# Pulling the second attention forward and laying the weights' pieces along both attentions

One core of one Trainium2 chip; the metric is the device time of one launch in microseconds (us), median of several runs.

## The reference

Four batches of 1088 tokens with 4 heads of 32 go through a polynomial-sketch attention and then through a mixing over tokens. Cut to what matters:

```python
def phi(x):                                  # 8 x 8 products of two sketches
    a = np.einsum('rd,bhsd->bhsr', S1, x)
    b = np.einsum('rd,bhsd->bhsr', S2, x)
    return np.einsum('bhsi,bhsj->bhsij', a, b).reshape(*x.shape[:-1], r * r)
q_p, k_p = phi(q), phi(k)
num = np.einsum('bhsf,bhfd->bhsd', q_p, np.einsum('bhsf,bhsd->bhfd', k_p, v))
den = np.einsum('bhsf,bhf->bhs', q_p, np.sum(k_p, axis=2))[..., None] + 1e-06
x = num / den                                # then, heads side by side:
theta = x @ w_theta
y = einsum('ts,bsd->btd', w_tok_r, x*cos(theta)) + einsum('ts,bsd->btd', w_tok_i, x*sin(theta))
u = x + y
out = u + maximum(u @ w_ch, 0)
```

Two 1088 x 1088 token weights are needed by every mixing. They arrive as 64-bit floats in 34 pieces of 128 x 544.

## The kernel before

A scheduler puts each engine's instructions in an order by the levels' priorities and its own estimates of time; the program text only gives dependencies and priorities. A piece of the weights takes one transfer, three ScalarE passes and two VectorE instructions:

```python
        A.activation(dst, hi.bitcast(F32), AF.Copy, scale=2.0**-112)
        A.activation(step[:, :, 1].bitcast(F16), hi.bitcast(F32), AF.Copy, scale=2.0**-60)
        A.activation(step[:, :, 0], lo.bitcast(U32), AF.Copy, scale=2.0**-29)
        ts(x, x, 3, ALU.logical_shift_left)
        tt(V, x, x, step.rearrange("p n t -> p (n t)").bitcast(I32), ALU.add)
```

An attention is, in this order of data: powers of keys and queries (a maximum over the block, a trip through TensorE and back), slices of keys and queries, a small matrix, `features` (`lv`), `denominators` (first instruction `fl`, last `rd`), and for each of three token groups the query product `qp`, its transposes and products on TensorE, `x`, and cosine and sine parts `z`. The level "first" goes before "weights", and "attention" after it:

```python
    with level("weights"):
        for i in range(NK):
            for n in range(0, S, PIECE):
                load_f32(wT[:, i, n:n + PIECE], w_tok[i][:, n:n + PIECE])
    # ... cut ...
    with level("first"):
        # ... constants, first keys ...   (cut)
        attention(0)
    with level("attention"):
        keys(1)
        attention(1)
        keys(2)
    mixing(0, True)                       # all three token groups at once
    # ... mixings 1 to 3 between attentions 2 and 3 (cut)
```

Of the kernel before, what the change touches and what calls it, by code (L numbers as in the profile page):

```python
# [21 lines left out]
F32 = mybir.dt.float32  # L22
F16 = mybir.dt.float16
# [15 lines left out]
TINY = 2.0**-60  # L39
PIECE = 544  # L40
# [3 lines left out]
def kernel(  # L44
# [46 lines left out]

    def tt(eng, o, a, b, op):
        eng.tensor_tensor(out=o, in0=a, in1=b, op=op)  # L93

    def ts(o, a, s1, op0, s2=None, op1=None):
        kw = {} if op1 is None else {"op1": op1}
        V.tensor_scalar(out=o, in0=a, scalar1=s1, scalar2=s2, op0=op0, **kw)  # L97

    def stt(o, a, s, b, op0, op1):
        V.scalar_tensor_tensor(out=o, in0=a, scalar=s, in1=b, op0=op0, op1=op1)  # L100

# [16 lines left out]
    def load_f32(dst, src):  # L118
# [13 lines left out]
        step = stg.tile([P, PIECE, 2], I16, tag="step", name="step", bufs=2)[:p, :n]  # L132
# [4 lines left out]
        ts(x, x, 3, ALU.logical_shift_left)  # L137
        tt(V, x, x, step.rearrange("p n t -> p (n t)").bitcast(I32), ALU.add)

    def load_pair(src, n, tag, copies=1):  # L140

        p = src.shape[0]
        m = p * copies
        hi = const.tile([P, n], F32, tag=f"{tag}_hi", name=f"{tag}_hi")[:m]
        lo = const.tile([P, n], F32, tag=f"{tag}_lo", name=f"{tag}_lo")[:m]
        if src.dtype == F32:
            for i in range(copies):
                nc.sync.dma_start(hi[i * p:(i + 1) * p], src)
            V.memset(lo, 0.0)
            return hi, lo  # L150
        st = const.tile([P, n], I64, tag=f"{tag}_st", name=f"{tag}_st")[:m]
        for i in range(copies):
            nc.scalar.dma_start(st[i * p:(i + 1) * p], src)
        wl, wh = split(st)
        x = magnitude(hi, wh)
        y = const.tile([P, n], I32, tag=f"{tag}_y", name=f"{tag}_y")[:m]
# [4 lines left out]
        z = const.tile([P, n], I32, tag=f"{tag}_z", name=f"{tag}_z")[:m]  # L161
# [29 lines left out]
    def absmax(o, a, axis=AX.X):  # L191
        V.tensor_reduce(out=o, in_=a, axis=axis, op=ALU.max, apply_absolute_value=True)

# [25 lines left out]
    def cut4(dst, x0, rest, c0, c1, near=1, p=P):  # L219
# [3 lines left out]
        r = sm.tile([P, (B - 1) * P], F32, tag="cut_r", name="cut_r", bufs=1)[:p, :n]  # L223
        z = sm.tile([P, (B - 1) * P], F32, tag="cut_z", name="cut_z", bufs=1)[:p, :n]
# [19 lines left out]
    def spread(m, cs, z):  # L244

        o = m[:, :, cs].rearrange("p l (h r) -> p l h r", h=H)
        for o_, z_, f in ((o[:, 0:4], z, hmf[:, 0:4]), (o[:, 4:6], z[:, 0:2], hmf[:, 4:6])):
            n = o_.shape[1]
            tt(V, o_, z_.unsqueeze(2).to_broadcast([P, n, H, R]),
               f.unsqueeze(3).to_broadcast([P, n, H, R]), ALU.mult)  # L250
# [14 lines left out]
    for b in range(B):  # L265
# [6 lines left out]


    def keys_slices(b):

        kn = tiles["k", b]
# [4 lines left out]
        tt(V, ipk[:, b, 1], ip, ip, ALU.mult)  # L281

# [31 lines left out]
    def keys_matrix(bs, cm):  # L314
# [48 lines left out]
        cut4([nz[:, i].rearrange("p b r -> p (b r)") for i in range(NL)], nl[:, 0], by_level(nl), *UNIT)  # L363
        for i, b in enumerate(bs):
            spread(mv[b], slice(2 * HR, 3 * HR), nz[:, :, i])
# [4 lines left out]
        ts(g[:, 0], g[:, 0], sab[:, 0:1], ALU.mult)  # L370

    def keys_values(b, pool=(ps_acc, "acc")):

        kn, vn = tiles["k", b], tiles["v", b]
        kv = psum(*pool)[:, :4 * D].rearrange("p (n d) -> p n d", n=2)
        for g in range(NG):
# [10 lines left out]
            ks = work.tile([P, CH, 2 * R], F32, tag="ks", name="ks")  # L387
            A.copy(ks.rearrange("p n r -> p (n r)"), kf)
            kp = work.tile([P, CH, R, R], F32, tag="feat", name="kp")
# [9 lines left out]
        for j in range(2):  # L399
            pj = slice(j * R * R, (j + 1) * R * R)  # L400
            A.copy(kvbd[b][pj, :, j * D:(j + 1) * D], kv[pj, :, j * D:(j + 1) * D])
# [4 lines left out]
    def query_slices(b):  # L406

# [7 lines left out]
        tiles["qs", b] = qs  # L415
        qx = work.tile([P, NC * P], F32, tag="qx", name="qx", bufs=1)
        sl = [work.tile([P, NC * P], F16, tag=f"q{i}", name=f"q{i}", bufs=1) for i in range(3)]
        half = work.tile([P, NC * P], F16, tag="half", name="half", bufs=1)
        for g in range(NG):
            tr = psum(ps_w, "w")  # L420
# [6 lines left out]
        ts(sl[0], qx, 1.5 * 2.0**24, ALU.add, 1.5 * 2.0**24, ALU.subtract)  # L427
        tt(V, qx, qx, sl[0], ALU.subtract)
        ts(half, qx, 1.5 * 2.0**12, ALU.add, 1.5 * 2.0**12, ALU.subtract)
        A.activation(sl[1], half, AF.Copy, scale=2.0**10)  # L430
        tt(V, qx, qx, half, ALU.subtract)
        A.activation(sl[2], qx, AF.Copy, scale=2.0**10)
        tiles["qsl", b] = sl

    def features(b):

        sl, m = tiles["qsl", b], mv[b]
        lv = work.tile([P, NL, 3, NC, HR], F32, tag="lv", name="lv", bufs=1)
        W = 3 * HR
        for c in range(NC):  # L440
            lp = psum(ps_w, "w")[:, :NL * W]
            q0, q1, q2 = (x[:, c * P:(c + 1) * P] for x in sl)
            flat = m.rearrange("p l n -> p (l n)")
            nc.tensor.matmul(lp, q0, flat[:, 0:4 * W], start=True, stop=False, skip_group_check=True)  # L444
            nc.tensor.matmul(lp[:, W:], q1, flat[:, 0:3 * W], start=False, stop=False, skip_group_check=True)
            nc.tensor.matmul(lp[:, 2 * W:], q2, flat[:, 4 * W:6 * W], start=False, stop=True, skip_group_check=True)  # L446
            A.copy(lv[:, :, :, c].rearrange("p l t n -> p (l t) n"),  # L447
                   lp.rearrange("p (x n) -> p x n", n=HR))
        tiles["lv", b] = lv

    def denominators(b):
        lv = tiles["lv", b].rearrange("p l t c n -> p l t (c n)")
        fl = work.tile([P, 3, NT], F32, tag="fl", name="fl", bufs=1)
# [284 lines left out]
```

## Time and profile before

| | us |
|---|---|
| median of 4 runs beside the changed kernel | 354.18 (352.19 to 355.84) |
| first z of batch 0, of batch 1 | 117.45, 190.22 |
| last piece of the weights | 109.65 |

The prediction below shows the strip, the busy times by stretch (busy us and number of instructions by engine, the granted clock of TensorE, the DMA engines' busy share, GB/s), the pieces' groups and the chain. Two more views matter later. First the busy times in two stretches (busy us and number of instructions by engine, the granted clock of TensorE, the DMA engines' busy share, GB/s):

```profile
core 0: us, PE busy (x) PEld busy (x) DVE busy (x) ACT busy (x) POOL busy (x), PEclk, DMA share, GB/s
44.00:105.00 61.00, 22.19 (x99) 17.30 (x99) 49.26 (x140) 49.76 (x85) 0.00 (x0) 0.53 0.59 203
105.00:165.00 60.00, 53.95 (x277) 38.16 (x278) 39.49 (x112) 26.86 (x55) 0.00 (x0) 0.85 0.10 30
```

VectorE is busy 88.75 of the 121 us from 44 to 165. Second, four of its instructions in the order of time (start, us):

```profile
42.24 1.36 DVE L93 TENSOR_TENSOR qx<-qx,half 128x1152 f32<-128x1152 f32 x1
...
63.78 1.34 DVE L192 TENSOR_REDUCE m<-ld_q 128x4 f32<-128x1152 f32 x1
...
92.78 0.95 DVE L93 TENSOR_TENSOR qp<-fl 128x768 f32<-128x768 f32 x1
...
105.02 0.37 DVE L490 RECIPROCAL rd<-dn 128x36 f32<-128x36 f32 x1
```

These are the subtraction for the third slice of batch 0's queries, the maximum over *batch 1's* queries, the first query product of batch 0, and the reciprocal that nearly ends its denominators. Batch 1's maximum runs ahead of batch 0's query product, and the query product ahead of the reciprocal: the two batches, and the stages of one, overlap in VectorE's queue.

### The profile page before, as it was taken

To read this page: it belongs to the slowest core of one execution; us is meant where nothing else is said; L and a number is where in the kernel's file an instruction comes from. 1 tells how busy PE (TensorE), PEld (TensorE's weight loads), DVE (VectorE), ACT (ScalarE), POOL (GpSimd) and SP (SyncE) were. 2 spreads that over 40 slices of the span, in tenths; PEclk is the share of its full clock that TensorE was granted. 3 is DMA by queue.
4 is the path that set the end of the run, shared out by engine and by line. 5 is a ranking of instruction groups with operands and counts; after the bars stand their busy time and mean duration, and the time that the engine had idled before them with its cause. 6 is when DMAs were issued, how large, how long until landed. Compare 5 with 4: busy or idle time off the path is not lost.

```text
span 354.1 us, 4014 instructions
## 1 busy us (share of the span) xinstructions
PE 271.9 (77%) x1355; PEld 191.3 (54%) x1355; DVE 237.8 (67%) x681; ACT 167.0 (47%) x333; POOL 0.7 (0%) x6
## 2 busy tenths in 40 slices
PE   0406680127236799999978999999999999999994
PEld 0304480014125576675646778567776866776662
DVE  4897868884998178748986576887769289332111
ACT  0799839999955556043113365132456320442000
POOL 0000000000000000000000000000000000000000
PEclk9999955556555599999987999999999999999998
DMA  7668519884800004010010014000000000000000
GB/s 276 228 236 280 168 62 311 274 297 149 274 22 1 2 1 136 0 67 1 2 44 19 2 67 129 6 23 24 1 19 2 0 24 0 23 20 0 22 22 19
DMA packets 11604, 28.78 MB, mean 81 GB/s; under 512 B 1216, under 2 KB 5568, under 8 KB 11584
## 3 DMA queue, kind: packets, MB, share of 16 engines
q1 hardware_dynamic: 11376, 28.51, 24.1%
q8 instruction: 10, 0.16, 0.2%
q14 instruction: 10, 0.08, 0.1%
q10 hardware_dynamic: 208, 0.02, 0.0%
HBM read 26.30 MB, written 2.23 MB: 81 GB/s over the span
## 4 chain that ended last, share of the span: by engine, by line
PE 62%; DVE 17%; ACT 13%; DMA 4%; issue 1%; ACTq 0%; SPq 0%
PE y L560 31%; PE w L513 5%; ACT step L135 3%; PE acc L395 3%; ACT step L136 3%; PE w L533 3%; PE y L395 2%; PE w L507 2%; ACT lv L447 2%; PE y L570 2%; DVE wT L93 2%; PE w L385 2%; DMA s_t_st<-s_t 2%; ACT wT L134 2%; DVE kx L93 1%
## 5 line engine op out<-in xcount | busy, mean ns | idle before, releaser
L560 PE MATMUL y<-wT,zst 128*128 128x384 f32 (+1 forms) x384 | 134.9, 482 | 2.0 <-DVE zst L93 1.9
L560 PEld LDWEIGHTS y<-wT,zst 128*128 128x128 f32 x384 | 68.7, 193 | 32.2 <-DVE zst L93 3.2
L579 ACT COPY ot<-y 128x384 f32<-128x384 f32 (+2 forms) x16 | 5.9, 398 | 58.3 <-PE y L574 53.9
L135 ACT ACTIVATE step<-st 128x544 f16<-128x544 f32 (+1 forms) x35 | 27.8, 794 | 6.0 <-DVE wT L93 6.0
L513 PEld LDWEIGHTS w<-kvbd,qpT 128*128 128x128 f32 x144 | 22.0, 217 | 13.0 <-ACT qpT L511 11.0
L136 ACT ACTIVATE step<-st 128x544 int16<-128x544 uint32 (+1 forms) x35 | 27.5, 786 | 0.0
L93 DVE CUSTOM_DVE_ANT_0 wT<-wT,step 128x1088 uint16<-128x1088 uint16 x34 | 24.4, 718 | 4.5 <-ACT step L136 3.8
L513 PE MATMUL w<-kvbd,qpT 128*128 128x64 f32 x144 | 24.4, 305 | 3.8 <-ACT qpT L511 3.7
L134 ACT ACTIVATE wT<-st 128x544 f32<-128x544 f32 x34 | 23.2, 685 | 2.0 <-DMA st<-w_tok 1.9
L93 DVE TENSOR_TENSOR uT<-xT,y 128x384 f32<-128x384 f32 (+1 forms) x12 | 6.3, 528 | 22.5 <-PE y L560 22.5
L511 ACT COPY qpT<-w 128x256 f32<-128x256 f32 x36 | 12.7, 368 | 18.0 <-PE w L507 17.5
L507 PE MATMUL w<-ident,qp 128*128 128x128 f32 x72 | 14.0, 299 | 7.9 <-DVE qp L93 7.9
L530 ACT COPY xT<-w 128x384 f32<-128x384 f32 x12 | 5.7, 476 | 25.2 <-PE w L528 25.2
L100 DVE SCALAR_TENSOR_TENSOR tt<-tn,w 128x384 f32<-128x384 f32 x12 | 6.6, 552 | 14.9 <-ACT tn L537 14.9
L447 ACT COPY lv<-w 128x384 f32<-128x384 f32 x36 | 14.9, 499 | 2.9 <-PE w L446 2.9
L97 DVE TENSOR_SCALAR wT<-wT 128x544 int32<-128x544 int32 x34 | 14.6, 434 | 1.7 <-ACT wT L134 1.6
L507 PEld LDWEIGHTS w<-ident,qp 128*128 128x128 f32 x72 | 9.9, 168 | 8.9 <-ACT wT L134 7.9
L93 DVE TENSOR_TENSOR kp<-ks 128x768 f32<-128x768 f32 x12 | 11.4, 953 | 4.5 <-PE acc L395 2.5
L444 PE MATMUL w<-mv,q 128*128 128x384 f16 x36 | 13.2, 368 | 0.9 <-DVE mv L93 0.9
L395 PEld LDWEIGHTS acc<-ld_v,kp 128*128 128x128 f32 x108 | 13.1, 192 | 1.5
L93 DVE TENSOR_TENSOR zst<-x,tn 128x384 f32<-128x384 f32 (+1 forms) x12 | 6.1, 512 | 11.3 <-ACT tn L540 11.3
L533 PEld LDWEIGHTS w<-w,xT 128*128 128x128 f32 x72 | 10.7, 215 | 5.0 <-ACT xT L530 4.4
(228 smaller groups left out, 503.8 us busy)
## 6 DMA issues: line engine op xcount, KB each, us to landing
st<-w_tok SPq DMA_DIRECT2D x34, 544.0 KB, 4.6
ld_k<-k_l SPq DMA_DIRECT2D x4, 576.0 KB, 4.0
ld_q<-q_l SPq DMA_DIRECT2D x4, 576.0 KB, 4.3
ld_v<-v_l SPq DMA_DIRECT2D x4, 576.0 KB, 3.6
out<-ot SPq DMA_DIRECT2D x8, 192.0 KB, 2.1
out<-ot SPq DMA_DIRECT2D x4, 128.0 KB, 1.8
st<-w_sq SPq DMA_DIRECT2D x1, 256.0 KB, 4.5
out<-ot SPq DMA_DIRECT2D x4, 32.0 KB, 1.9
```

Source lines behind the costliest of these rows:

```text
L93: eng.tensor_tensor(out=o, in0=a, in1=b, op=op)
L97: V.tensor_scalar(out=o, in0=a, scalar1=s1, scalar2=s2, op0=op0, **kw)
L134: A.activation(dst, hi.bitcast(F32), AF.Copy, scale=2.0**-112)
L135: A.activation(step[:, :, 1].bitcast(F16), hi.bitcast(F32), AF.Copy, scale=2.0**-60)
L136: A.activation(step[:, :, 0], lo.bitcast(U32), AF.Copy, scale=2.0**-29)
L395: nc.tensor.matmul(kv[:, n], kp[:, i * H + 2 * n:i * H + 2 * n + 2].rearrange("p h i j -> p (h i j)"), vn[:, c, 2 * n:2 * n + 2].rearrange ...
L444: nc.tensor.matmul(lp, q0, flat[:, 0:4 * W], start=True, stop=False, skip_group_check=True)
L447: A.copy(lv[:, :, :, c].rearrange("p l t n -> p (l t) n"), lp.rearrange("p (x n) -> p x n", n=HR))
L507: nc.tensor.transpose(tr[:, n * P:(n + 1) * P], qp[:, i * H + 2 * n:i * H + 2 * n + 2].rearrange("p h i j -> p (h i j)"), ident)
L513: nc.tensor.matmul(num[:, i * P + n * 2 * D:i * P + (n + 1) * 2 * D], qpT[:, n], kvbd[b][:, n], start=True, stop=True)
L533: nc.tensor.matmul(th[:, i * P:(i + 1) * P], xT[:, i * P:(i + 1) * P], w2[:, 0], start=True, stop=True)
L560: nc.tensor.matmul(yp[:, :t1 - t0], z, wT[:, i, t0:t1], start=(i == 0), stop=(i == NK - 1))
```

## The change

An *order edge* is a dependency that puts one instruction behind another in VectorE's queue, and no data passes along it. The intent: let the second attention follow the first at once, so that VectorE and ScalarE work on it while TensorE mixes batch 0; spread the pieces evenly along both attentions' VectorE work; and mix all three token groups row by row as the rows of the weights come. A list `along` takes up each VectorE instruction of the two attentions with an estimated size; piece *j* gets a place on that scale. Its two instructions go behind the attentions' instruction below the place (called the **lower edge** here), and the attentions' first instruction more than `SLACK` above the place goes behind the piece (the **upper edge**). The edges only give an order within VectorE. The core of the diff:

```diff
+FIRST, SLACK = 4000, 3000
+    def note(x, speed=1):
+        if state.cur_priority < levels["weights"]:
+            along.append((last_on_dve(), 140 + math.prod(x.shape[1:]) / speed))
+    def interleave(first, slack):
+        at, total = [], 0
+        for ins, w in along:
+            total += w
+            at.append((total, ins))
+        step = (total - first) / (len(rows) // 2)
+        for j in range(len(rows) // 2):
+            p = first + j * step
+            low = [i for t, i in at if t <= p]
+            high = [i for t, i in at if t > p + slack]
+            for ins in rows[2 * j:2 * j + 2]:
+                if low:
+                    behind(ins, low[-1])
+            if high:
+                behind(high[0], rows[2 * j + 1])
...
-        step = stg.tile([P, PIECE, 2], I16, tag="step", name="step", bufs=2)[:p, :n]
+        step = stg.tile([P, PIECE, 2], I16, tag="step", name="step", bufs=3)[:p, :n]
...
+    order = [j * NF + i for i in range(NF) for j in range(2)] + [NK - 1]
...
     with level("first"):
...
+        with tc.issue_after(tiles["ready", 0]):
+            features(0)
+            keys_values(0, spare)
+            denominators(0, 0, NC)
+            for g in range(NG):
+                mixed(0, g, numerator(0, g))
+            load(1, "kqv")
+            keys_powers(1)
+            query_powers(1)
+            keys_slices(1)
+            matrices(1)
+            query_slices(1, (ps_acc, "acc"))
+        keys_features(1)
+        keys_values(1)
+        attention(1)
+        interleave(FIRST, SLACK)
     with level("attention"):
-        keys(1)
-        attention(1)
         keys(2)
```

Left out: small constants loaded and cut together, two key-value matrices in place of four, key features split from key-value products, and a tile of its own for batch 0's z.

## The prediction

> **What bounds the kernel now.** I read the views in this order: the page's strip of 40 slices, busy time by stretch, the groups, the waits, the chain, and the order in time around 118 us. The strip first, because the kernel has two regimes:
>
> ```profile
> PE   0406680127236799999978999999999999999994
> DVE  4897868884998178748986576887769289332111
> ACT  0799839999955556043113365132456320442000
> PEclk9999955556555599999987999999999999999998
> ```
>
> One digit is about 8.85 us. To about slice 13 VectorE (DVE) and ScalarE (ACT) are nearly full and TensorE (PE) mostly waits at a clock of one half. From there on PE is full. The same in numbers, by stretch:
>
> ```profile
> core 0: us, PE busy (x) PEld busy (x) DVE busy (x) ACT busy (x) POOL busy (x), PEclk, DMA share, GB/s
> 0.00:44.00 44.00, 15.98 (x76) 10.98 (x76) 34.00 (x148) 30.82 (x57) 0.70 (x6) 1.00 0.71 237
> 44.00:118.00 74.00, 29.37 (x126) 22.68 (x126) 58.82 (x157) 58.69 (x101) 0.00 (x0) 0.52 0.49 168
> 118.00:177.00 59.00, 58.48 (x308) 40.46 (x309) 41.55 (x113) 20.12 (x44) 0.00 (x0) 0.96 0.10 31
> 177.00:200.00 23.00, 19.36 (x95) 13.59 (x94) 15.25 (x52) 7.76 (x20) 0.00 (x0) 0.85 0.08 24
> 200.00:354.00 154.00, 148.70 (x753) 103.56 (x753) 88.20 (x215) 49.64 (x115) 0.00 (x0) 0.99 0.07 23
> ```
>
> After 118 us PE is busy 58.48 + 19.36 + 148.70 = 226.5 of 236 us; only 9.5 us are idle. Before it, PE is busy 45.4 of 118. So the end is set by **when PE can start its dense part**, plus 226.5, plus the idle time inside it. What opens that part is the first z of batch 0, which lets the first mixing begin:
>
> ```profile
> 115.51 1.28 ACT L540 ACT_TABLE_LOAD   x1
> 117.45 0.56 DVE L93 TENSOR_TENSOR zst<-x,tn 128x384 f32<-128x384 f32 x1 [3.28 <-ACT tn L540]
> 118.07 2.93 PE L560 MATMUL y<-wT,zst 128*128 128x384 f32 x4 [1.41 <-DVE zst L93]
> ```
>
> Why it comes only at 117.5: the first attention shares DVE and ACT with all 34 pieces of the token weights. Each piece takes three ACT and two DVE instructions, and the last one is done at about 110 us, ahead of z:
>
> ```profile
> L135 ACT ACTIVATE step<-st 128x544 f16<-128x544 f32 x34 | 27.3, 804 | 6.0 <-DVE wT L93 6.0
> L136 ACT ACTIVATE step<-st 128x544 int16<-128x544 uint32 x34 | 27.0, 795 | 0.0
> L134 ACT ACTIVATE wT<-st 128x544 f32<-128x544 f32 x34 | 23.2, 685 | 2.0 <-DMA st<-w_tok 1.9
> L93 DVE CUSTOM_DVE_ANT_0 wT<-wT,step 128x1088 uint16<-128x1088 uint16 x34 | 24.4, 718 | 4.5 <-ACT step L136 3.8
> L97 DVE TENSOR_SCALAR wT<-wT 128x544 int32<-128x544 int32 x34 | 14.6, 434 | 1.7 <-ACT wT L134 1.6
> ```
>
> By the starts in the order of time a piece occupies ACT for 1.89 us (64.54 to 66.43) and DVE for 0.35 + 0.64 = 1.0 us, so 64 us of ACT and 34 us of DVE in all. In the chain the largest entry is the mixing itself, and nothing of the loading of the weights' pieces by DMA carries weight:
>
> ```profile
> PE y L560 31%; PE w L513 5%; ACT step L135 3%; PE acc L395 3%; ACT step L136 3%; PE w L533 3%; PE y L395 2%; PE w L507 2%; ACT lv L447 2%; PE y L570 2%; DVE wT L93 2%; PE w L385 2%; DMA s_t_st<-s_t 2%; ACT wT L134 2%; DVE kx L93 1%
> ```
>
> **What the Trainium skill says.** "Perfetto Trace Analysis", section Optimization Strategy: where the most contended engine changes over time, interleaving the regimes can help. The stretches above are such a case, and the change does just that. "TensorE: Matmul & The Clock Gate", Part 1: the array runs at half clock after an idle window of about 3.4 us and at full clock after sustained work. The trace agrees in part: 0.52 in 44 to 118 with PE waiting, and full again from about 123, some 5 us after dense work began; but in 0 to 44 the granted clock is 1.00 although PE is busy only 36%, which that rule doesn't give. The same page (Part 1, engine queue depths) says that ACT and DVE are strict FIFO and that PE's matmuls keep their order. So an instruction that is early in a queue and not ready holds what is behind it; the waits fit (ACT waited 6.0 us for wT's last DVE step with other work behind it).
>
> **The change part by part.**
>
> *Sizes.* 34 pieces before and after, the same four attentions, the same 204 mixing matmuls. The number of DVE rows falls from 645 to 621: small constants now go together (96 columns in place of two sets), two key-value matrices instead of four, two copies fewer; the doubled 1152-wide product becomes two of 576. Adding up start-to-start costs of all rows (1152-wide product 1.27 us, 576-wide 0.67, shift 0.35, addition of a piece 0.64, tiny ones 0.085) gives 205 us after against 207 before. So 2 us of work go; the rest is order.
>
> *First z.* Before, all 34 pieces precede the first z; after, 16 do, by the order of the DVE queue. Summed in that way, the work ahead of the first z is 62 us. For before the same sum up to the last piece is 83 us where the trace shows 88 us busy, a factor of 1.06; so 66 us. To this comes idle time. Before, DVE sat idle 5 us in the first 10 and 17 us in the next 100. The chain of small steps through the matrices (powers, cuts, each through PE and back) has fewer fillers now, so I don't take less than its share: about 9 us more to z. **First z at 66 + 5 + 9 = 80 us**, 37 us earlier than 117.5.
>
> *PE after the first z.* The same work remains at that moment as before: four mixings, three attentions, all outputs and the rest of attention 0, measured 226.5 us. With no more idle time than before the end would be 80 + 226.5 + 9.5 = 316 us.
>
> *What is added: a shared stretch.* Between the first z and the last piece three engines now have about the same work. DVE: 127.7 - 62.4 = 65 us in the sum, times 1.06, 69 us. ACT: 18 pieces of 1.89 = 34 us, a second attention of about 22 (its share of the 167 us that ACT is busy in all, less the pieces), and two groups of the first's tail of about 3 each: 62 us. PE: the mixing of batch 0, 17 rows of 3 groups, two records each at 0.32 us (36 records in 11.6 us at full clock; 0.27 for the 320-wide), 31 us; attention 1 about 26 (its matmuls at full-clock spacing); the tail of attention 0 about 6; outputs 3; first keys of batch 2 about 2: 68 us. Each row of the mixing waits for its piece, and attention 1's matmuls stand in the same PE queue. Three queues with 62 to 69 us of work that wait for each other do not run at 100%; at 85% the stretch lasts about 80 us instead of 69, and PE loses about 80 - 68 = 12 us where it lost little before. Half of that I expect to get back, for two reasons: the 3.6 us of idle time and the dip of the clock in 177 to 200, where mixing 0's outputs, attention 1 and mixing 1 queued up for DVE, should mostly go; and some PE work of batch 2 can be pulled in. So plus 6.
>
> *Sum:* 80 + 226.5 + 9.5 + 6 = **322 us**, 31 us or 8.8% less than 353.1. The last piece ends at about 160 us, 50 us later than before, and that hurts nothing by itself, since only mixing 0 needs it.
>
> *The rest.* z of batch 0 gets a tile of its own instead of two staging buffers, so it needn't wait for the pieces to leave them; three step buffers instead of two take away part of ACT's 6.0 us wait. The start loses ScalarE's DMA issues; its table load waited 8.0 us for such a DMA, but DVE's first work (absolute maximum at 4.77) didn't, so 1 to 2 us at most. Both are within the 9 us above.
>
> **The rivals.**
>
> *Rival A: the shared stretch becomes bound by PE at half clock.* If PE's gaps in 80 to 160 keep the clock at 0.5 to 0.6, 68 us of work takes 115 us or more, z of batch 1 comes late, and the gain shrinks to about 37 - (115 - 80) = nothing to 10 us: 340 to 350. For it: 44 to 118 runs at 0.52 at 40% busy, and 177 to 200 at 0.85 even at 84% busy. Against it: PE has some 85% to do here, and dense work brought the clock back within 5 us at 118.
>
> *Rival B: the first attention is a chain of latencies.* Then taking the pieces out of its way gains little: DVE idles in their place and the first z comes at 95 to 100; end at about 337. For it: DVE waited 4.3 us for PE just before the denominators, and PE's longest waits (11.3, 10.6, 9.0) are for small DVE steps. Against it: the wait of 10.6 was long because DVE had pieces in between (by the order in time, 17 of the 34 additions stand among the small steps from 48 to 80 us).
>
> *Rival C: the order fits better than I think.* First z at 72 and no new idle time: 72 + 226.5 + 8 = 306. For it: pieces are spread by the amount of DVE work, with slack, as one would after tuning. Slower than before would need PE to lose over 37 us of new waiting; nothing speaks for it but a queue in bad order.
>
> **Range and chances.** C gives the low end, B the high one: 306 to 338 should hold it 8 times in 10. A beyond 346 (2%) needs both a late first z and a clock at half: 5% for within 2% and slower together.
>
> **What would show it right or wrong.** Right: the first mixing matmul at about 80 us (72 to 92); PE's busy time from there about 226 us, idle 10 to 20 us, most of it before the last piece at about 160; granted clock above 0.8 from 90 us on; from 165 us PE over 97% busy. Rival A shows as a clock below 0.7 in 90 to 160, B as DVE below 75% busy in 20 to 80 and a first z after 92. Wrong altogether: PE idle over 25 us after the first z, waiting for pieces (DVE wT) while DVE waits for ACT, or ACT full in the shared stretch.

## The result, and the profile after

| | before | after |
|---|---|---|
| median us (4 runs each, same chip) | 354.18 (352.19 to 355.84) | 368.36 (366.41 to 368.46) |
| first z of batch 0 / of batch 1 | 117.45 / 190.22 | 106.95 / 193.23 |
| last piece of the weights | 109.65 | 202.01 |
| TensorE busy / idle from first z to the end | 226.5 / 10.1 | 237.8 / 21.7 |

The ratio is 1.039 (95% interval 1.0319 to 1.0461): **slower**, where 322 us were predicted (306 to 338, and a chance of 5% for "within 2% and slower together"). Against the kernel before, first z comes 10.5 us earlier, but TensorE is then busy 11.2 us longer and idle 11.6 us longer. A ratio is the mean time of one kernel's fast runs over that of the other's fast runs of the same rounds, so not quite the ratio of the medians. Executions over 1.5% slower than the fastest of the same kernel are left out of the means. The strip after (a digit is 9.16 us):

```profile
PE   2735216630679998594889999999899999999994
DVE  5497778459527568888978987499748469332011
ACT  2799444574566943576345440620435431442000
PEclk9999855565557999788569999999989999999998
```

Counting slices from 0, TensorE stands in slice 9 (82 to 92 us), starts its dense part after it, and has a second hole in slices 15 to 20. VectorE isn't full any more in slices 7 to 14, where it was mostly at 8 or 9 before; the exception is slice 9, in which TensorE waits for it. The stretches that answer to those of before:

```profile
44.00:105.00 61.00, 26.31 (x112) 20.51 (x112) 40.08 (x107) 31.04 (x54) 0.00 (x0) 0.53 0.33 101
105.00:165.00 60.00, 52.67 (x256) 35.47 (x256) 43.06 (x114) 39.05 (x70) 0.00 (x0) 0.87 0.37 118
165.00:200.00 35.00, 26.86 (x124) 17.67 (x122) 29.73 (x62) 17.53 (x35) 0.00 (x0) 0.76 0.08 26
```

From 44 to 105 us VectorE is busy 40.1 us where it was 49.3, although it was to be given *more* to choose from. ScalarE is busy 31.0 us where it was 49.8, and no engine is full. From 165 to 200 TensorE is busy 77%. The chain is the mixing, as before, and the longest wait of TensorE and the pieces' groups are:

```profile
PE y L624 33%; PE w L568 5%; DVE wT L127 4%; PE acc L449 3%; PE w L597 3%; PE w L431 2%; PE w L501 2%; PE y L634 2%; PE y L449 2%; PE w L562 2%; DVE lv L127 2%; DVE wT L132 2%; PE w L502 2%; PE w L592 1%; PE acc L349 1%
```

```profile
PE w L562 <- DVE dn L127: 16.6, 1, 16.6
...
PE y L624 <- DVE wT L127: 6.2, 6, 1.6
```

```profile
L624 PE MATMUL y<-wT,z 128*128 128x384 f32 (+1 forms) x120 | 52.6, 558 | 7.7 <-DVE wT L127 6.2
...
L172 ACT ACTIVATE step<-st 128x544 f16<-128x544 f32 (+1 forms) x35 | 28.3, 807 | 25.0 <-DVE wT L127 19.9
...
L171 ACT ACTIVATE wT<-st 128x544 f32<-128x544 f32 x34 | 23.2, 693 | 15.1 <-DMA st<-w_tok 14.9
```

(The waits list gives us in total, times, longest.) TensorE stands 16.6 us once, ahead of the transposes of the first query product (L562), and only 6.2 us for rows of the weights in the mixing (L624). ScalarE waits 19.9 us for a piece's buffer where it waited 6.0. VectorE in the order of time shows what the 16.6 us are:

```profile
65.58 0.28 DVE L244 TENSOR_REDUCE mx<-acc 4x1 f32<-4x128 f32 x1 [1.82 <-PE acc L242]
65.78 0.70 DVE L127 CUSTOM_DVE_ANT_0 wT<-wT,step 128x1088 uint16<-128x1088 uint16 x1
66.42 1.34 DVE L127 TENSOR_TENSOR qx<-qx,half 128x1152 f32<-128x1152 f32 x1
...
77.14 1.06 DVE L136 SCALAR_TENSOR_TENSOR fl<-lv 128x864 f32<-128x864 f32 x1 [4.50 <-ACT lv L504]
...
92.05 0.95 DVE L127 TENSOR_TENSOR qp<-fl 128x768 f32<-128x768 f32 x1
...
93.37 0.37 DVE L550 RECIPROCAL rd<-dn 128x36 f32<-128x36 f32 x1
...
106.95 0.56 DVE L127 TENSOR_TENSOR z<-x,tn 128x384 f32<-128x384 f32 x1 [3.74 <-ACT tn L604]
...
129.24 1.35 DVE L232 TENSOR_REDUCE m<-ld_q 128x4 f32<-128x1152 f32 x1
```

Read it against the four lines of before. The query's third slice starts at 66.4 (42.2 before), behind a piece's addition, itself behind a step that waited for TensorE. The query product needs `fl` only, yet stands at 92.05, at the very end of the denominators (1.3 us ahead of the reciprocal; 12 us before). Batch 1's query maximum, which needs only its load (that of the keys ran at 60.1), stands at 129.24, behind all of batch 0's z; before it ran at 63.8. **Much of the overlap is gone from the queue.** Whether that is the cause is what the experiments ask.

### The profile page after: what moved, and what is told of

Its sections match the earlier page's. It is cut to its first block, busy times and chain, and to the rows that moved or that the text cites. A ratio compares the mean times of both kernels' runs of the same rounds, so it can differ in the third digit from the quotient of the medians.

```text
span 366.4 us, 3992 instructions
## 1 busy us (share of the span) xinstructions
PE 284.3 (78%) x1355; PEld 197.0 (54%) x1355; DVE 240.3 (66%) x663; ACT 168.8 (46%) x331; POOL 0.7 (0%) x6
## 4 chain that ended last, share of the span: by engine, by line
PE 67%; DVE 22%; ACT 6%; issue 3%; DMA 1%; SPq 0%; ACTq 0%
PE y L624 33%; PE w L568 5%; DVE wT L127 4%; PE acc L449 3%; PE w L597 3%; PE w L431 2%; PE w L501 2%; PE y L634 2%; PE y L449 2%; PE w L562 2%; DVE lv L127 2%; DVE wT L132 2%; PE w L502 2%; PE w L592 1%; PE acc L349 1%
## 5 line engine op out<-in xcount | busy, mean ns | idle before, releaser
L624 PE MATMUL y<-wT,zst 128*128 128x384 f32 (+1 forms) x288 | 98.6, 476 | 0.8 <-DVE zst L127 0.8
L624 PEld LDWEIGHTS y<-wT,zst 128*128 128x128 f32 x288 | 51.8, 192 | 25.0 <-DVE zst L127 1.2
L624 PE MATMUL y<-wT,z 128*128 128x384 f32 (+1 forms) x120 | 52.6, 558 | 7.7 <-DVE wT L127 6.2
L172 ACT ACTIVATE step<-st 128x544 f16<-128x544 f32 (+1 forms) x35 | 28.3, 807 | 25.0 <-DVE wT L127 19.9
L624 PEld LDWEIGHTS y<-wT,z 128*128 128x128 f32 x120 | 23.5, 220 | 20.8 <-DVE wT L127 10.8
L568 PEld LDWEIGHTS w<-kvbd,qpT 128*128 128x128 f32 x144 | 23.9, 232 | 12.2 <-ACT qpT L566 9.1
L562 PE MATMUL w<-ident,qp 128*128 128x128 f32 x72 | 14.0, 311 | 20.4 <-DVE dn L127 16.6
L568 PE MATMUL w<-kvbd,qpT 128*128 128x64 f32 x144 | 25.7, 320 | 3.1 <-ACT qpT L566 3.0
L562 PEld LDWEIGHTS w<-ident,qp 128*128 128x128 f32 x72 | 10.2, 173 | 21.2 <-issue 21.2
L501 PE MATMUL w<-mv,qsl 128*128 128x384 f16 x36 | 13.5, 390 | 7.2 <-DVE mv L127 7.0
L431 PEld LDWEIGHTS w<-s_bd,kT 128*128 128x128 f32 x72 | 11.0, 225 | 7.2 <-ACT kT L428 5.2
L431 PE MATMUL w<-s_bd,kT 128*128 128x64 f32 x72 | 12.2, 314 | 2.4 <-ACT kT L428 1.2
```

Source lines behind the costliest of these rows:

```text
L431: nc.tensor.matmul(kf[:, i * H * 2 * R:(i + 1) * H * 2 * R], kT[:, i], s_bd.rearrange("p h r -> p (h r)"), start=True, stop=True)
L501: nc.tensor.matmul(lp, q0, m[:, 0:4 * W], start=True, stop=False, skip_group_check=True)
L562: nc.tensor.transpose(tr[:, n * P:(n + 1) * P], qp[:, i * H + 2 * n:i * H + 2 * n + 2].rearrange("p h i j -> p (h i j)"), ident)
L568: nc.tensor.matmul(num[:, i * P + n * 2 * D:i * P + (n + 1) * 2 * D], qpT[:, n], kvbd[b % 2][:, n], start=True, stop=True)
L624: nc.tensor.matmul(yp[:, :t1 - t0], z, wT[:, i, t0:t1], start=(n == 0), stop=(n == NK - 1))
```

## The experiments

All are edits of the changed kernel. Medians of 4 runs; "ratio" is against the kernel before in the same rounds (its median there was 353.1 to 353.9). Positions in us are from one profiled execution each: the subtraction for batch 0's third query slice, the maximum over batch 1's queries, the first z of batch 0, the first z of batch 1, and VectorE's busy time from 44 to 165.

| run | us | ratio | third slice | maximum | first z | z of 1 | DVE busy |
|---|---|---|---|---|---|---|---|
| e1 no laying | 337.40 | 0.951 | 29.0 | 67.9 | 104.2 | 173.1 | 102.9 |
| e5 lower edges only | 337.42 | 0.954 | 29.0 | 58.8 | 92.3 | 160.5 | 103.5 |
| e12 lower edges, tighter | 338.13 | 0.957 | 29.2 | 62.0 | 92.8 | 170.0 | 103.1 |
| e6 upper edges only | 339.37 | 0.959 | 44.8 | 76.7 | 110.1 | 170.9 | 105.6 |
| e8 pieces behind first z | 341.62 | 0.966 | 31.0 | 50.3 | 79.4 | 162.4 | 105.8 |
| e15 upper edges 19 to 33 | 342.44 | 0.970 | 29.0 | 59.2 | 91.5 | 168.9 | 100.6 |
| e10 wide slack | 348.11 | 0.986 | 38.9 | 84.4 | 92.1 | 170.5 | 99.4 |
| e9 own order only | 350.81 | 0.991 | 65.2 | 124.0 | 105.5 | 184.3 | 91.4 |
| e13 lower edges + own order | 355.32 | 1.005 | 55.3 | 115.6 | 94.1 | 183.0 | 91.2 |
| e18 upper edge behind the shift | 367.12 | 1.034 | 60.9 | 122.2 | 101.3 | 186.2 | 86.2 |
| changed kernel | 368.36 | 1.039 | 66.4 | 129.2 | 107.0 | 193.2 | 83.1 |
| e14 upper edges 0 to 18 | 375.14 | 1.061 | 66.6 | 133.2 | 110.5 | 199.4 | 81.5 |

(The full conversion work is done in all of these.) The table is sorted by time, and the last column falls with it nearly row by row: what a version loses is VectorE time left idle between 44 and 165 us. That is a correlation; the runs below take it apart.

### Which part of the change costs: e1 to e4

**e1, no laying.**

```diff
-        interleave(FIRST, SLACK)
```

> The changed kernel without the laying-out of the weights' pieces: the second attention stays right behind the first, the pieces go where their priority puts them (24 of 34 additions ahead of the first attention's last steps, 25 before its first z). Theory 1 (the even laying is what costs: it spreads the last row to 180 us, so that the first mixing waits row by row in the tensor queue at half clock): first z later than 107 us, about 115, but hardly a wait of the mixing for pieces after it; total at or below the kernel before, 345 to 355. Theory 2 (the second attention among the first mixing is what costs, through the queues in order): about as slow as the change, 362 to 372.

Measured 337.4 us (335.86 to 338.59), ratio 0.951 (0.9445 to 0.9571). Without laying the change is a gain of 16 us; the laying turns it into a loss of 14.

**e2, the second attention back at the later level, the pieces laid along the first only.** `interleave` is called right behind attention 0, and batch 1 stands in `level("attention")`.

```diff
+        interleave(FIRST, SLACK)
+    with level("attention"):
             load(1, "kqv")
             keys_powers(1)
...
         attention(1)
-        interleave(FIRST, SLACK)
-    with level("attention"):
         keys(2)
```

> The second attention goes back to its old level, behind everything of the first; the pieces are laid evenly along the first attention alone. Theory 1 (laying costs by where the last row lands): the last piece lands near the first z again, so about 350 to 356. Theory 2 (the second attention costs): also about 350 to 356. Theory 3 (the rearranged start of the first attention itself, its chain through the engines, costs): first z not before 107 us and total over 358.

Measured 361.2 us, ratio 1.016 (1.0104 to 1.0225). TensorE's wait for the query product is there again (17.4 us), and the third slice stands at 72.1.

**e3, both: second attention later and no laying.** As e2, and:

```diff
-        interleave(FIRST, SLACK)
```

> Neither of the two: second attention at its old level, no laying. What is left of the change is the rearranged start, the own tile for z and the order of the rows. If these are harmless: 350 to 356 like the kernel before. If the start or the rows' order cost or gain: away from 354 by that much, and the same offset is in all kernels of the change.

Measured 352.42 us, ratio 0.993 (0.9877 to 0.9981). The four corners: neither 352.4, laying alone 361.2 (+9), second attention early alone 337.4 (-15), both 368.4. With the second attention early the laying costs 31 us, more than three times what it costs along one attention alone. From e3, which still has the small regroupings, the kernel before differs by under 1%, so those aren't the subject.

**e4, rows of the weights in plain order.**

```diff
-    order = [j * NF + i for i in range(NF) for j in range(2)] + [NK - 1]
+    order = list(range(NK))
```

> The whole change, but the rows of the weights loaded and mixed in their old order 0 to 16 and not in pairs of real and imaginary. If the pairing matters for when the mixing can begin: the first mixing still begins with row 0, so within 1% of the change, 365 to 371. Clearly lower would say that the paired order costs.

Measured 369.24 us, ratio 1.041 (1.0341 to 1.0469): the order of the rows is irrelevant.

### Late pieces, or what else in the laying: e5 to e8

**e5, lower edges only.** A piece waits for its place; nothing waits for a piece.

```diff
-            if high:
-                behind(high[0], rows[2 * j + 1])
```

> The laying with one of its two edges: a piece may not come ahead of its place along the attentions, but attention no longer has to stay behind a piece. Theory L (holding the pieces back is what costs: ScalarE's part and the loads stand still behind four staging buffers, and the last row comes late): about as slow as the change, 360 to 370, last addition of a piece after 160 us. Theory H (holding attention behind pieces is what costs, by waits of the vector engine for ScalarE and the loads): at the level of the second attention alone, 336 to 345.

Measured 337.42 us (337.28 to 338.91), ratio 0.954 (0.9487 to 0.959). Busy times of this run in the two stretches, its instructions in the order of time, and its mixing group:

```profile
44.00:105.00 61.00, 37.21 (x204) 28.29 (x205) 52.53 (x144) 37.90 (x70) 0.00 (x0) 0.67 0.36 112
105.00:165.00 60.00, 50.72 (x253) 34.64 (x253) 50.99 (x127) 43.28 (x81) 0.00 (x0) 0.86 0.38 123
```

```profile
28.97 1.34 DVE L125 TENSOR_TENSOR qx<-qx,half 128x1152 f32<-128x1152 f32 x1
...
58.82 1.34 DVE L230 TENSOR_REDUCE m<-ld_q 128x4 f32<-128x1152 f32 x1
...
67.83 0.95 DVE L125 TENSOR_TENSOR qp<-fl 128x768 f32<-128x768 f32 x1
...
81.53 0.36 DVE L548 RECIPROCAL rd<-dn 128x36 f32<-128x36 f32 x1
...
92.28 0.56 DVE L125 TENSOR_TENSOR z<-x,tn 128x384 f32<-128x384 f32 x1 [2.26 <-ACT tn L602]
```

```profile
L622 PE MATMUL y<-wT,z 128*128 128x384 f32 (+1 forms) x120 | 46.9, 503 | 5.6 <-DVE wT L125 5.6
```

VectorE is busy 103.5 of 121 us, 20 more than in the changed kernel, with the same work in all. Its last piece is at 170.4, some 10 us later than the prediction had it; e12 will show that this does no harm. The wait for rows is 5.6 us, as in the changed kernel (6.2), so that wait isn't the difference. The same 120 matmul records of the mixing (102 of them batch 0's) take 46.9 us in place of 52.6.

**e6, upper edges only.**

```diff
                 if low:
-                    behind(ins, low[-1])
+                    pass
```

> The other edge alone: pieces may come as early as they like, attention stays behind a piece that is late by more than the slack. Since pieces run ahead by their priority, the edge should seldom bind. Theory L: like the second attention alone, 335 to 343. Theory H: 350 or more.

Measured 339.37 us, ratio 0.959 (0.9539 to 0.9641). So either kind of edge alone is harmless, and only the two together cost 31 us. Of the causes I had in mind none predicts that, except one: a lower and an upper edge on the same piece *chain the attentions' own instructions to each other*, through the piece.

**e7, the first mixing takes row 0 of the weights for all rows** (wrong, relative error 0.226), so that it waits for no late piece.

```diff
-                nc.tensor.matmul(yp[:, :t1 - t0], z, wT[:, i, t0:t1], ...
+                nc.tensor.matmul(yp[:, :t1 - t0], z, wT[:, i if b else 0, t0:t1], ...
```

> Wrong result on purpose: the whole change, but the first mixing multiplies by row 0 of the weights in every step, so that it waits for no later row. Theory P (the first mixing waits in the tensor queue for late rows, and holds the second attention behind it): the second attention's first z moves from 193 us to 165 or less, the total to 345 or less. Theory D (the pieces laid along the second attention slow it by themselves, in the vector and scalar queues): total within 2% of the change, 360 to 370.

Measured 373.04 us, ratio 1.051 (1.0437 to 1.0584), the first z of batch 1 at 193.6 as in the changed kernel. It isn't faster at all: that the mixing waits for late pieces is refuted as the cause.

**e8, all pieces behind the first z** by lower edges to it, no upper edges.

```diff
-        interleave(FIRST, SLACK)
+        for ins in rows:
+            behind(ins, tiles["z0"])
```

> The change with all pieces held back behind the first z of batch 0 on the vector engine (and no other edge). My prediction took the first z for set by the vector engine's work ahead of it: with no piece ahead, the sum is 51 us (62 in the change), so the first z would come at 75 us or earlier. Rival theory (a chain of latencies through tensor, scalar and vector engine sets it): 95 to 105 us, with the vector engine under 65% busy up to there. The total will be slow either way, over 360, because all rows come after it.

Measured 341.62 us, ratio 0.966 (0.9603 to 0.9709). First z at 79.4 with no piece ahead, where e5 has it at 92.3 with about half of them: the pieces do hold up the first attention. But what is gained there is lost behind it (from first z to first z of batch 1 83.0 us, against 68.2 in e5): VectorE does the pieces in one place or in the other. Two of the figures I expected were misses: first z at 75 us or earlier, and a total over 360 us.

### The order among the attentions' own instructions: e9 to e12

With 34 places and a step of some 2770 units, `SLACK` of 3000 makes the upper instruction of place *j* nearly the lower one of place *j* + 1. `along` is in the order of the program text. The pairs of edges thus turn the text's order into VectorE's order, about every 2770 units: attention 0 to its end, then batch 1. This binds the upper instructions alone: batch 1's key maximum, which is not one of them, still runs at 60.1 in the changed kernel. Worked out from the kernel's text, place 9 puts the third query slice behind batch 0's small matrix, places 14 to 16 put the query products behind the denominators and the z before them, and place 18 puts batch 1's query maximum behind the third z.

**e9, that order alone.** No piece is laid.

```diff
-            for ins in rows[2 * j:2 * j + 2]:
-                if low:
-                    behind(ins, low[-1])
-            if high:
-                behind(high[0], rows[2 * j + 1])
+            if low and high:
+                behind(high[0], low[-1])
```

> No piece is laid anywhere; only the order edges remain that the two-sided laying makes in passing: for each of its 34 places, the attentions' own instruction above the place is put behind the own instruction below it. The query products of the first attention again lie behind the middle of the denominators (in the listing before the chip: second product behind the reciprocal; without any laying all three before it), and the power of batch 1's queries behind the third z. Theory O (the loss of 31 us is the order that the pairs of edges force on the attentions' own instructions, not the pieces): well above the 337 us of the kernel without laying, 350 to 370 us, with PE's wait for the query product at 12 us or more again. Theory L (the pieces themselves, held in two-sided slots, stretch the attentions): 335 to 342 us, as without laying.

Measured 350.81 us (349.11 to 351.04), ratio 0.991 (0.9873 to 0.9943). That is 13 us more than e1 without any piece laid, so the order is a cause; the 31 us aren't reached. Its VectorE order has the third slice and batch 1's maximum as late as the changed kernel has them, with no piece laid:

```profile
65.23 1.35 DVE L124 TENSOR_TENSOR qx<-qx,half 128x1152 f32<-128x1152 f32 x1
...
87.92 0.95 DVE L124 TENSOR_TENSOR qp<-fl 128x768 f32<-128x768 f32 x1
...
93.13 0.37 DVE L547 RECIPROCAL rd<-dn 128x36 f32<-128x36 f32 x1
...
124.04 1.35 DVE L229 TENSOR_REDUCE m<-ld_q 128x4 f32<-128x1152 f32 x1
```

**e10, a wider slack.**

```diff
-FIRST, SLACK = 4000, 3000
+FIRST, SLACK = 4000, 12000
```

> Both edges stay for all 34 places, but the upper bound is taken 12000 units above the place instead of 3000, some four steps later, so that an upper bound no longer is the neighbour of the lower one, and the pairs of edges put few own instructions in order (in the listing the three query products come before the reciprocals again). Theory O: 336 to 348 us. Theory L: pieces are still held on both sides, so 355 to 368 us.

Measured 348.11 us, ratio 0.986 (0.9818 to 0.9897), at the edge of what the order theory gave. Twenty of the 31 us go, with all 34 lower and nearly all upper bounds in force.

**e11, no upper edge at places 14 to 18**, which hold back the query products and batch 1's query power.

```diff
-            if high:
+            if high and not 14 <= j <= 18:
```

> The upper bound is left out at five of the 34 places only (14 to 18: those that hold back the three query products of the first attention, one z, and the power of batch 1's queries); the other 29 keep both edges, and from batch 1's key products on DVE's own order in the listing is that of the changed kernel. Theory O with the damage done in the first attention: 336 to 348 us, the wait of PE for the query product gone, first z before 100 us. If the order is to blame but the damage is spread over both attentions: 350 to 362 us. Theory L: 362 to 368 us.

Measured 360.43 us (median of four, one of them slow; ratio of the fast ones 1.017, interval 1.0113 to 1.0221). Eight us come back. My idea that these five edges do the damage was wrong; the harm is spread wider. The order in the queue is fixed in the program: its trace has all three query products ahead of the reciprocal and batch 1's maximum ahead of batch 0's `fl`, as the kernel before has them, and the third slice still behind the small matrix (place 9 keeps its pair). So these visible signs, put right at five places, are not what makes up most of the loss.

**e12, lower edges only, steps three quarters as long**, to beat e5.

```diff
-        step = (total - first) / (len(rows) // 2)
+        step = 0.75 * (total - first) / (len(rows) // 2)
```

> A version to beat both: only the lower edge (a piece is held back, nothing waits for a piece), with steps three quarters as long, so that the last piece may come at some 145 us instead of 170. In the run with lower edges alone the output of batch 0's mixing followed right on the last piece (169.5 and 170.4 us); if that bound, this gives 330 to 336 us with first z at 93 to 97 us; if the pieces only move from one place beside the attentions to another, 336 to 340 us.

Measured 338.13 us, ratio 0.957 (0.9531 to 0.9599): no better. The last piece is at 137.5 in place of 170.4, and the time is the same.

### How much is order, and where: e13 to e18

**e13, lower edges for the pieces, and the own order beside them,** with no piece between.

```diff
-            if high:
-                behind(high[0], rows[2 * j + 1])
+            if low and high:
+                behind(high[0], low[-1])
```

> Each piece waits for its lower instruction, and no instruction waits for a piece; beside that each upper instruction is put behind the lower one directly, so that the attentions' own instructions stand in the order of the changed kernel (in the listing the query products lie among and behind the reciprocals, and batch 1's query power behind the z, as there). Theory O (order alone): 360 to 370 us, first z at 102 to 108 us. Theory M (order costs the 13 us of the run with order edges only, the rest comes from pieces in slots of VectorE's queue): 348 to 354 us.

Measured 355.32 us (353.86 to 357.31), ratio 1.005 (0.9972 to 1.0125). Against e5 the order costs 18 us. That is 1.3 us above the range of theory M and 4.7 us below that of theory O: the order is a large part, and a rest of 13 us is left in the changed kernel. In the order of time:

```profile
55.27 1.35 DVE L127 TENSOR_TENSOR qx<-qx,half 128x1152 f32<-128x1152 f32 x1
...
94.11 0.56 DVE L127 TENSOR_TENSOR z<-x,tn 128x384 f32<-128x384 f32 x1 [2.75 <-ACT tn L604]
...
115.60 1.35 DVE L232 TENSOR_REDUCE m<-ld_q 128x4 f32<-128x1152 f32 x1
```

First z is within 2 us of e5's; batch 1's maximum is 57 us later than there, and the first z of batch 1 comes 22.5 us later. So in these traces the order's cost appears behind first z, in batch 1, which stands behind batch 0. What the changed kernel has on top lies ahead of first z: third slice at 66.4 in place of 55.3, first z 12.8 us later, and from there on the two kernels run alike (259.5 us to the end against 261.1).

**e14, upper edges at places 0 to 18 only; e15, at 19 to 33 only.**

```diff
-            if high:
+            if high and j <= 18:        # e14;   j >= 19 in e15
```

> Both edges as in the changed kernel for places 0 to 18, those of the first attention; from 19 on only the lower edge. If the damage is done up to the first attention's z: 355 to 368 us with first z at 104 to 108 us. If it is done in the second: 340 to 348 us.

> The other part of the upper edges: both edges for places 19 to 33, only the lower edge before. The run with the upper edges at places 0 to 18 took 375 us, more than the changed kernel. If the damage lies in those places alone: 335 to 344 us, first z at 91 to 95 us. If the two parts each do harm: 346 to 356 us.

Measured 375.14 us for e14, ratio 1.061 (1.0546 to 1.0674), and 342.44 us for e15, ratio 0.970 (0.9614 to 0.9782). The damage is done by the pairs of edges of places 0 to 18, the last of which is the one that holds back batch 1's query maximum. Those of the second attention cost at most 5 us without the others, and with them nothing.

**e16 and e17, without the pieces' additions**, 34 VectorE instructions that cost 0.64 us each from start to start, 22 us in all; e16 is the changed kernel, e17 the one with lower edges only. (The result is wrong: relative error 1.02, not "by little" as I wrote.)

```diff
-        tt(V, x, x, step.rearrange("p n t -> p (n t)").bitcast(I32), ALU.add)
```

> The changed kernel without the additions by which each piece gets its low bits: 34 of VectorE's instructions of 0.72 us fewer, with a starting distance of 0.64 us, so 22 us of its time (result wrong by design, by little; the own instructions stand in the order of the changed kernel in the listing). Theory O, in which VectorE stands idle for order's sake: the time falls by far less than 22 us, to 352 to 365 us. If VectorE's load bounds here: 340 to 350 us.

> The same additions taken away from the kernel with the lower edges alone (337 us). If VectorE's load bounds the two attentions there, as its busy share of 85% from 44 to 165 us suggests: 318 to 326 us. If something else bounds them: 330 to 337 us.

Measured 345.19 us for e16 and 325.54 us for e17 (ratios 0.977 and 0.920). The edit takes away more than VectorE's load. ScalarE no longer waits for a piece's buffer (no such wait is left in either trace; it was 19.9 us in the changed kernel and 8.7 in e5), and in e16 the upper instructions wait for the piece's shift only, as in e18 below. So e17 fits VectorE's load bounding e5 in part (22 us less load, 12 us less time), but doesn't part it from ScalarE's wait. e16 is a miss: I expected that an engine idle for order's sake would gain little, and it gained 23 us. Between e16 and e17 the pairs of edges still cost 20 us, which is near the 18 in e13 against e5, although in e16 the pairs still go through the shift; the 11 us more that the additions' absence gave is about the rest of 13.

**e18, the upper edge behind a piece's first instruction only.**

```diff
-                behind(high[0], rows[2 * j + 1])
+                behind(high[0], rows[2 * j])
```

> Both edges for all 34 places, but the upper instruction waits only for the piece's first instruction (the shift, which needs one ScalarE pass) and no longer for its addition (which needs all three). The own order is the changed kernel's. If what own instructions wait for behind a piece is its addition: 352 to 359 us, as with the order alone (355). If the pair of edges as such does it: 363 to 370 us.

Measured 367.12 us (363.18 to 368.7), ratio 1.034 (1.0248 to 1.0436). One of the four is slow. In its profiled run, the fastest, the third slice is at 60.9 and the first z at 101.3, each some 5.5 us earlier than in the changed kernel, yet the median hardly moved (fast runs alone 366.78). So it isn't enough to free the own instructions from the addition.

## Why the prediction was wrong, point by point

**The sum, term by term.** The profiled execution lasts 366.4 us, 44.4 more than 322: first z came 27.0 later than 80, TensorE was busy 11.2 longer from there than 226.5, and idle 6.2 longer than 9.5 + 6. So the step that failed most is first z, and in it the idle time; what the prediction left out is the order that the pairs of edges give to the attentions' own instructions.

**"So 2 us of work go; the rest is order."** True, and the place where I stopped looking. I took the order that the edges give to the *pieces* into account and not the order that they give to everything else. The listing of VectorE's order could be built before the chip was used and shows it (query product by the reciprocal, batch 1's maximum behind the z); I used it for sums only.

**"First z at 66 + 5 + 9 = 80 us"** failed: 107. Busy times up to first z, of the changed kernel, e5, e13 and e8:

```profile
0.00:106.95 106.95, 46.53 (x193) 34.75 (x193) 70.60 (x236) 62.94 (x110) 0.70 (x6) 0.71 0.48 156
0.00:92.28 92.28, 43.48 (x215) 32.88 (x216) 74.75 (x246) 57.21 (x102) 0.70 (x6) 0.76 0.50 163
0.00:94.11 94.11, 44.81 (x193) 32.94 (x193) 72.21 (x237) 59.22 (x105) 0.70 (x6) 0.87 0.50 164
0.00:79.41 79.41, 41.55 (x202) 31.47 (x203) 60.12 (x214) 31.55 (x64) 0.70 (x6) 0.77 0.29 98
```

With the 16 pieces ahead that I counted, VectorE is busy 70.6 us (66 predicted) and idle 36.4 (5 + 9 = 14 predicted). The idle time was the mis-sized term. In e5, with 16 pieces ahead too, it is 17.5 us and in e13 21.9, so what the changed kernel has on top of e13 is 14.5 us of idle time and no work.

The runs split the 27 us also by edges. With *no* piece ahead of first z it comes at 79.4 (e8), so the 80 left no room for the 16 pieces that I counted; with lower edges it comes at 92.3 (e5): 13 us. The own order adds 2 (94.1 in e13), and own instructions behind pieces add 13 (107.0). The changed kernel shows both signs named for rival B: VectorE busy 42.5 of the 60 us from 20 to 80 (71%), and first z after 92. But the reason given for B, a chain of latencies that leaves nothing to gain, is refuted by e8's 79.4. B's price, 337 us, is e5's time and not the changed kernel's.

**"Slower would need PE to lose over 37 us of new waiting"** took the 37 us gained at first z for certain. First z came only 10.5 us earlier, and 11.6 us of new idle time with 11.2 us of longer busy time were enough. "A queue in bad order", named there as the one thing that could speak for it, is what came.

**"PE after the first z: 226.5 us"** holds in e5: TensorE is busy there 226.4 us from first z to the end and idle 16.8 (predicted 9.5 + 6), and 92.3 + 226.4 + 16.8 = 335.5, the span of that run. So the prediction's sum describes e5, with a first z 12 us too early. That it agrees to 0.1 us is luck: how much work is left at first z depends on the order (221.8 us in e1, 233.2 in e8). In the changed kernel TensorE is busy 237.8 us. Half of the 11 us is the same 120 matmul records of the mixing at 558 ns against 503. The granted clock was 0.78 from 105 to 125 and 0.67 from 165 to 185, where part of them ran; how much of it is the clock wasn't taken apart.

**"A shared stretch at 85%, plus 6 us"** failed in the changed kernel: from first z to the last piece it took 95.1 us where 80 were predicted, and 78.1 in e5. What was late was not the pieces' feeding but batch 1: from first z to batch 1's first z it took 86.3 us, in e5 68.2. e13 against e5 shows that the own order alone does it (88.9). The idle time of TensorE from first z on was mis-sized less, 21.7 us for 15.5.

**"Three step buffers take away part of ACT's 6.0 us wait"** failed: the wait rose to 19.9 us (8.7 in e5, 13.7 in e13).

**"Rows that come late"**, the sign "TensorE idle over 25 us after first z, waiting for pieces": it was idle 21.7 us, but only 6.2 for pieces, and e7 shows that nothing is gained where it needn't wait for them.

**Rival A** (half clock): its sign, a clock below 0.7 from 90 to 160, didn't come; it was 0.78. The clock was low where TensorE was busy less (0.53 from 44 to 105 with 26.3 of 61 us busy, 0.76 from 165 to 200 with 26.9 of 35). That this is a consequence of the waits more than a cause is argued; no run holds the clock fixed.

The balance of the 31 us between e5 and the changed kernel: 18 by the own order (e13 against e5; 13 without laid pieces, e9 against e1), shown. The other 13 arise ahead of first z, only with both edges *through* the pieces, as idle time of VectorE, and are also about what removing the additions gave beyond its share. The trace shows the third slice late behind an addition that stands behind a step waiting for TensorE; that this placing, a decision of the scheduler under both edges, makes the 13 us is argued, and e18 did not confirm it. A rival that no run tests is ScalarE: ahead of 107 us it waits 10.8 us for pieces' buffers in the changed kernel and 10.6 in e18, but 3.4 in e13, and its other work stands behind these passes. The cause of the 13 us stays open, and so does why e14, with fewer edges, is slower than the changed kernel by 7 us.

**What the Trainium skill contributed.** "Perfetto Trace Analysis", section Optimization Strategy, says that interleaving regimes may improve performance. e1 against e3 agrees with that (337.40 against 352.42 us). "TensorE: Matmul & The Clock Gate", Part 1, says that ScalarE and VectorE take their queues strictly in order; the trace fits: TensorE stood 16.6 us, and the query product it stood for ran 10 us after its input was last written (at 81.35), with denominators ahead of it in the queue.

The prediction set one figure against the rule of the clock, and misread it: the granted clock of 1.00 from 0 to 44 us in the kernel before. The same kind of matmul started every 0.53 us there and every 0.27 us at 123 us, so it ran at half its later rate while the record said 1.00:

```profile
31.46 0.53 PE L303 MATMUL y<-ksl 128*128 128x384 f16 x1
...
31.99 0.53 PE L303 MATMUL y<-ksl 128*128 128x384 f16 x1
...
123.38 0.33 PE L303 MATMUL acc<-ksl 128*128 128x384 f16 x1
...
123.65 0.33 PE L303 MATMUL acc<-ksl 128*128 128x384 f16 x1
```

This was no part of the sum.

## What to carry to other kernels

A pair of order edges "behind A, ahead of B" around filler work also orders B behind A. Along a list in program order it took away much of the overlap that the scheduler had found (18 us in e13 against e5). So hold fillers back from one side only (337.4 us here); a bound widened until it no longer met the next one gave back 20 of the 31 us, not all (e10). And compare the queue's listing of one's *own* instructions before and after, not only the place of what was moved; here it could have shown the changed order before any run, though not its price.

## What the Trainium skill lacked or had wrong

- "Perfetto Trace Analysis", Optimization Strategy: it says that interleaving regimes may help and lacks the warning that the means may cost more than the gain. The same interleaving gave 337.4 to 339.4 us with the order left free or bounded on one side, and 368.4 us bounded on both.
- "TensorE: Matmul & The Clock Gate", Part 1: beyond a general warning that records of the clock can be unreliable, it lacks that the record can stand at 1.00 at the start of a run while matmuls come at half their later rate. In e9 it is 1.00 from 44 to 75 us; the products of the query slices (a group of three) start 0.72 us apart up to 72.70 there and 0.36 us apart from 73.24 on. In e1 they start 0.72 us apart too (65.68 to 66.40), and the record says 0.50 from 60 to 70. So mean clocks of stretches near the start can't be compared between runs.
- No page has that order edges inside one engine's queue cost time with no work and no semaphore added: 13 us in e9 against e1, 18 us in e13 against e5.
